# A softmax reciprocal moved from ScalarE to VectorE, and the evacuations of V moved the other way

## The chip, the cores and the metric

The kernel runs on one core of a Trainium2 chip. The metric is the device time of one execution in microseconds (us). Five engines work side by side on a core: TensorE (PE: matmuls, PEld: its weight loads), VectorE (DVE), ScalarE (ACT), GpSimd (POOL) and SyncE (SP, which issues most DMAs). Matmul results land in PSUM, eight banks of 128 partitions; everything else lies in SBUF.

## The reference

Two layers run one after the other on x of 2048 x 512. The first is an attention with a memory of 8 rows that is carried from one segment of 32 rows to the next:

```
for s in range(64):                       # 2048 / 32 segments, in sequence
    h = concat([mem, xs])                 # 8 + 32 = 40 rows of the layer-normed x
    q, k, v = h @ Wq, h @ Wk, h @ Wv      # 32 heads of 128
    scores = where(mask, q @ k.T * scale, -1e9)
    p = softmax(scores)
    o = (p @ v) @ Wo
    mem = o[:8]; outs.append(o[8:])
h = x + concat(outs)
```

The second is a gated MLP: `z = gelu(layernorm(h) @ w_in)`, split into z1 and z2, `g = w_sp @ layernorm(z2) + b_sp`, and `out = h + (z1 * g) @ w_out`. The change concerns only the softmax of the first.

## The kernel before

The program is one list of operations, written out in order; each engine executes its own in that order. A small emitter records what each operation reads and writes and puts in the waits. PSUM banks are tracked as a whole: an operation that writes a bank waits for every earlier reader of it on another engine.

The loop over the 64 segments (lines 896 to 1025) cannot overlap the segments freely, since the memory rows that one segment makes are input to the next. Within a segment the 32 heads are done in two halves of 16, b = 0 and 1. The order on TensorE is:

1. Q and K of both halves (`QK`, L481), with ScalarE copying each result out (L488) and VectorE transposing it in blocks (L494, L497).
2. `S_half(0)`: the scores of half 0 into bank 0 (L511, L520, L526). ScalarE takes the exponential (`sm_exp`, L534) without subtracting a maximum: a constant shift is added instead.
3. `V_half(0)`: V of half 0 (L575) into bank 6, then `sm_sums(0)`: matmuls with a block matrix of ones (L541, L546) put the sums of the exponentials, repeated over the partitions of a head group, into columns 224 to 383 of bank 0.
4. `S_half(1)` into bank 1, three of the four steps of `V_half(1)` (bank 2), `sm_sums(1)` into bank 1, and the last step of `V_half(1)`.
5. One group of work from a queue `gx` (L411 or L430, or later `z2_group`, L735). These are projections for the memory rows of later segments, or early parts of the second layer; they need nothing of this segment and fill the time until P is normalised. For one segment, s = 48, no such group is left.
6. `PV_half(0)` and `PV_half(1)` (L592, L598). Each of them writes all four banks 0, 1, 6 and 7.
7. The context copies `cT_evac` (ScalarE L611, VectorE L613), the output projection (L625, and L676 for the other rows), and the new memory rows (L649, L654).

The reciprocal of the sums is made on ScalarE in two operations, a logarithm (`sm_ln`, L553, from PSUM) and an exponential of its negative (`sm_rcp`, L557). VectorE then multiplies it into the exponentials in two operations, 160 and 64 elements wide (`sm_norm`, L561 and L566). Both normalisations stand behind both V evacuations in the program. `V_evac(0)` is a VectorE copy (L584), `V_evac(1)` a ScalarE copy (L582). The factor 2^-64 in the logarithm, and the constants beside it, keep numbers in range; `UNSC` takes it out again in `cT_evac`.

Of the kernel before, what the change touches and what calls it, by code (L numbers as in the profile page):

```python
# [9 lines left out]
ACT = mybir.ActivationFunctionType  # L10
ALU = mybir.AluOpType
# [158 lines left out]
def fast_path(nc, st, keep, A_x, A_mem0, A_Wq, A_Wk, A_Wv, A_Wo, A_seg_len, B_w_in, B_w_sp, B_b_sp, B_w_out, out):  # L170
# [17 lines left out]
    scale = float(DH) ** -0.5  # L188
    EPS = 1e-5
    SHIFT = 44.0  # L190
    NEG = -1.0e30
    RBIAS = 44.42
    LNS = 2.0 ** -64
    RK = math.exp(-RBIAS)

    em = Emitter(n_dma_sems=40)

    def sb(name, shape, dt):
        return st.enter_context(nc.sbuf_tensor("f_" + name, shape, dt))
# [25 lines left out]
    E_sb = sb("E_sb", [128, 2, 224], BF)  # L225
    R_sb = sb("R_sb", [128, 2, 160], F32)
# [9 lines left out]
    ones = sb("ones", [128, 128], BF)  # L236
# [23 lines left out]
    ps = st.enter_context(nc.psum_tensor("f_ps", [128, 8, 512], F32))  # L260
# [5 lines left out]
    def PB(b):  # L266
        return ("ps", b)
# [4 lines left out]
    def pe(fn, **k):  # L272
        return em.add("pe", fn, **k)

    def act(fn, **k):
        return em.add("act", fn, **k)

    def dve(fn, **k):
        return em.add("dve", fn, **k)

    def pool(fn, **k):
        return em.add("pool", fn, **k)
# [40 lines left out]
    def late_consts():  # L323
        pool(lambda e: e.memset(ones[:], 0.0), writes=["ones"])
        pool(lambda e: e.memset(Sc[:], 0.0), writes=["Sc"])
        pool(lambda e: e.memset(mask[:], 0.0), writes=["mask"])
        for c in range(4):
            q = slice(32 * c, 32 * c + 32)
            pool(lambda e, q=q: e.memset(ones[q, q], 1.0), writes=["ones"])
            pool(lambda e, q=q: e.affine_select(out=G_sb[q, :], in_=onesrc[q, 0:M], pattern=[[-1, M]], compare_op=ALU.is_equal,  # L330
                                                fill=0.0, base=0, channel_multiplier=1), reads=["onesrc"], writes=["G"])
            pool(lambda e, q=q: e.affine_select(out=F_sb[q, :], in_=onesrc[q, 0:32], pattern=[[-1, 32]], compare_op=ALU.is_equal,
                                                fill=0.0, base=-M, channel_multiplier=1), reads=["onesrc"], writes=["F"])
            pool(lambda e, q=q: e.affine_select(
                out=Sc[q, :].rearrange("p (s r) -> p s r", r=32)[:, :, XM:32], in_=onesrc[q, 0:32].rearrange("p (s r) -> p s r", r=8),
                pattern=[[-8, 4], [-1, 8]], compare_op=ALU.is_equal, fill=0.0, base=0, channel_multiplier=1),
                reads=["onesrc"], writes=["Sc"])
            m1 = mask[q, 0:160].rearrange("p (g t) -> p g t", t=40)[:, :, 16:40]
            pool(lambda e, m1=m1: e.affine_select(out=m1, in_=m1, pattern=[[0, 4], [1, 24]], compare_op=ALU.is_ge,
                                                  fill=NEG, base=8, channel_multiplier=-1), reads=["mask"], writes=["mask"])  # L340
            m2 = mask[q, 160:224].rearrange("p (g t) -> p g t", t=16)
            pool(lambda e, m2=m2: e.affine_select(out=m2, in_=m2, pattern=[[-8, 4], [0, 16]], compare_op=ALU.is_ge,
                                                  fill=NEG, base=0, channel_multiplier=1), reads=["mask"], writes=["mask"])
            pool(lambda e, m2=m2: e.affine_select(out=m2, in_=m2, pattern=[[8, 4], [0, 16]], compare_op=ALU.is_ge,
                                                  fill=NEG, base=7, channel_multiplier=-1), reads=["mask"], writes=["mask"])
            m3 = m2[:, :, 0:8]
            pool(lambda e, m3=m3: e.affine_select(out=m3, in_=m3, pattern=[[8, 4], [1, 8]], compare_op=ALU.is_ge,
                                                  fill=NEG, base=0, channel_multiplier=-1), reads=["mask"], writes=["mask"])
# [32 lines left out]
    def slot(s):  # L381
        return s % NSLOT
# [154 lines left out]
    def sm_sums(b):  # L537
        bank = SBK[b]
        for c in range(4):
            q = slice(32 * c, 32 * c + 32)  # L540
            pe(lambda e, q=q, c=c: e.matmul(ps[q, bank, 224:384], lhsT=ones[:, q], rhs=E_sb[:, b, 0:160], start=True, stop=False,  # L541
                                            skip_group_check=True, tile_position=(0, 32 * c)),
               reads=[("E", b), "ones"], writes=[PB(bank)])
        for c in range(4):
            q = slice(32 * c, 32 * c + 32)
            pe(lambda e, q=q, c=c: e.matmul(ps[q, bank, 224:384].rearrange("p (g q) -> p g q", q=40)[:, :, 0:16], lhsT=ones[:, q],  # L546
                                            rhs=E_sb[:, b, 160:224].rearrange("p (g q) -> p g q", q=16), start=False, stop=True,
                                            skip_group_check=True, tile_position=(0, 32 * c)),
               reads=[("Ex", b), "ones"], writes=[PB(bank)])

    def sm_ln(b):
        bank = SBK[b]
        act(lambda e: e.activation(out=R_sb[:, b, :], in_=ps[:, bank, 224:384], func=ACT.Ln, scale=LNS),  # L553
            reads=[PB(bank)], writes=[("R", b)])

    def sm_rcp(b):
        act(lambda e: e.activation(out=R_sb[:, b, :], in_=R_sb[:, b, :], func=ACT.Exp, scale=-1.0, bias=RBIAS),  # L557
            reads=[("R", b)], writes=[("R", b)])

    def sm_norm(b):  # L560
        dve(lambda e: e.scalar_tensor_tensor(out=E_sb[:, b, 0:160], in0=R_sb[:, b, :], scalar=RK, in1=E_sb[:, b, 0:160],  # L561
                                             op0=ALU.mult, op1=ALU.mult),
            reads=[("R", b), ("E", b)], writes=[("E", b)])
        ev = E_sb[:, b, 160:224].rearrange("p (g q) -> p g q", q=16)
        rv = R_sb[:, b, :].rearrange("p (g q) -> p g q", q=40)[:, :, 0:16]
        dve(lambda e: e.scalar_tensor_tensor(out=ev, in0=rv, scalar=RK, in1=ev, op0=ALU.mult, op1=ALU.mult),  # L566
            reads=[("R", b), ("Ex", b)], writes=[("Ex", b)])

    def V_half(s, b, dcs=range(DC)):
        bank = VB[b]  # L570
        sl = slot(s)
        for dc in dcs:
            for c in range(4):
                c0 = (16 * b + 4 * c) * DH
                pe(lambda e, dc=dc, c=c, c0=c0: e.matmul(ps[32 * c:32 * c + 32, bank, :], lhsT=hT[:, sl, dc, :], rhs=w_v[:, dc, c0:c0 + 512],  # L575
                                                         start=(dc == 0), stop=(dc == DC - 1), tile_position=(0, 32 * c)),
                   reads=[("hTx", (s // 4) % 3), ("hTm", s, dc // 2), ("W", 2, 2 * b), ("W", 2, 2 * b + 1)], writes=[PB(bank)])

    def V_evac(b, eng):
        bank = VB[b]  # L580
        if eng == "act":
            act(lambda e: e.activation(out=V_sb[:, b, :], in_=ps[:, bank, :], func=ACT.Copy), reads=[PB(bank)], writes=[("V", b)])  # L582
        else:
            dve(lambda e: e.tensor_copy(out=V_sb[:, b, :], in_=ps[:, bank, :]), reads=[PB(bank)], writes=[("V", b)])  # L584
# [16 lines left out]
                start=False, stop=True, skip_group_check=True, tile_position=(32 * c, 0)),  # L601
                reads=[("Vx", xb), ("Ex", b)], writes=[PB(PVB[c])])

    UNSC = 2.0 ** -64


    def cT_evac(c, eng):
        src = ps[:, PVB[c], 0:320]
        dst = cT[:, c, :]
        if eng == "act":  # L610
            act(lambda e: e.activation(out=dst, in_=src, func=ACT.Copy, scale=UNSC), reads=[PB(PVB[c])], writes=[("cT", c)])  # L611
        else:
            dve(lambda e: e.tensor_scalar(out=dst, in0=src, scalar1=UNSC, scalar2=None, op0=ALU.mult),  # L613
                reads=[PB(PVB[c])], writes=[("cT", c)])
# [180 lines left out]
    def start_v(n):  # L795
        start_group(vx_mm, vx_evac, 0, n)
# [99 lines left out]
    for s in range(NSEG):  # L896
# [31 lines left out]
            for n in range(2, 4):  # L928
                start_v(n)
        V_half(s, 0)  # L930
        V_evac(0, "dve")
        sm_sums(0)
        sm_ln(0)
        S_half(s, 1)
        lastop["s"] = em.by_eng["pe"][-1]
        sm_exp(1)
        sm_rcp(0)
        if s == 0:
            for n in range(4, 8):
                start_v(n)  # L940
        V_half(s, 1, (0, 1, 2))
        sm_sums(1)
        sm_ln(1)
        sm_rcp(1)
        V_half(s, 1, (3,))
        lastop["v"] = em.by_eng["pe"][-1]
        if s == NSEG - 1:
            sp(lambda e: e.dma_start(w_in1, winr[:, :, 0:FH]), writes=["w_in1"], after=[lastop["s"], lastop["x"]])
            xn2T_dma(11, [lastop["s"], lastop["x"]])
            z2_back(0, 7, lastop["v"])  # L950
        V_evac(1, "act")
        sm_norm(0)
        sm_norm(1)
        if s + 1 < NSEG:
            qx_copy(s + 1)
            lastop["x"] = em.by_eng["pool"][-1]
# [6 lines left out]
        ev = [gx.pop(0)()] if gx else [z2_group()] if zx and s > 3 * CK else []  # L963
# [148 lines left out]
    def zbank():  # L1112
        zcnt[0] += 1
        return 5 + zcnt[0] % 3
# [22 lines left out]
    for k, rb in enumerate(range(NP, RB)):  # L1137
# [18 lines left out]
        if k in (2, 3):  # L1156
            r, j, bank = RB - 4 + k, (k - 1) % 2, zbank()
# [45 lines left out]
    for tb in range(NTB):  # L1203
        for fb in range(len(ACC) if tb == 0 else 0, FB):
            if tb == 0:
                bank = 5 + fb % 3
            else:
                bank = gcnt % 2
# [785 lines left out]
```

## Time and profile before

| | |
|---|---|
| median of 3 runs | 885.25 us (884.95 to 886.3) |
| the profiled execution | 887.59 us, span 885.8 us |
| mean granted clock of TensorE | 0.994 |
| busy share: PE, DVE, ACT, POOL | 97%, 55%, 52%, 12% |
| reciprocal on ACT (L553, L557) | 128 x 305 ns and 128 x 333 ns |
| normalisation on DVE (L561, L566) | 128 x 325 ns and 128 x 221 ns |
| V copy on DVE (L584), on ACT (L582) | 64 x 692 ns; 580 ns at 410.07 us |

Times in the profile count from the start of the span. A row of the timeline gives the start, the duration, the engine, the line of the program, the operation, what it writes and reads, and in brackets how long its engine had been idle before it and what it then waited for. A row of the groups gives a line's total busy time, the mean of one in ns, and the idle time before. A row of the windows gives, for a stretch of time, its length, the busy time of each engine with the number of instructions, the granted clock of TensorE as a share of full speed, the busy share of the DMA engines and the GB/s that they moved.

### The profile page before, as it was taken

To read this page: it belongs to the slowest core of one execution; us is meant where nothing else is said; L and a number is where in the kernel's file an instruction comes from. 1 tells how busy PE (TensorE), PEld (TensorE's weight loads), DVE (VectorE), ACT (ScalarE), POOL (GpSimd) and SP (SyncE) were. 2 spreads that over 40 slices of the span, in tenths; PEclk is the share of its full clock that TensorE was granted. 3 is DMA by queue.
4 is the path that set the end of the run, shared out by engine and by line. 5 is a ranking of instruction groups with operands and counts; after the bars stand their busy time and mean duration, and the time that the engine had idled before them with its cause. 6 is when DMAs were issued, how large, how long until landed. Compare 5 with 4: busy or idle time off the path is not lost.

```text
span 885.8 us, 46595 instructions
## 1 busy us (share of the span) xinstructions
PE 858.6 (97%) x21446; PEld 488.5 (55%) x21453; DVE 487.6 (55%) x1128; ACT 457.3 (52%) x1147; POOL 110.6 (12%) x280
## 2 busy tenths in 40 slices
PE   6889999999999999999999999999999998999997
PEld 6645555565566655656565555555555543444443
DVE  3445556565556556565655565556555557364343
ACT  2346565666665656666665666466665575400000
POOL 1420111111111111010101011111101013200000
PEclk9999999999999999999999999999999999999999
DMA  9962232123320311211312121523222299032101
GB/s 320 377 177 63 64 57 61 44 59 63 60 58 25 84 46 32 65 45 52 60 43 52 46 66 47 102 69 78 73 62 67 62 244 333 2 101 76 62 13 38
DMA packets 109210, 76.35 MB, mean 86 GB/s; under 512 B 64104, under 2 KB 94512, under 8 KB 109008
## 3 DMA queue, kind: packets, MB, share of 16 engines
q1 hardware_dynamic: 108496, 73.04, 30.1%
q8 instruction: 170, 2.79, 1.3%
q14 instruction: 32, 0.26, 0.1%
q0 software_dynamic: 192, 0.20, 0.1%
q10 hardware_dynamic: 320, 0.07, 0.0%
HBM read 41.75 MB, written 20.91 MB: 71 GB/s over the span
## 4 chain that ended last, share of the span: by engine, by line
PE 94%; DVE 2%; issue 1%; DMA 1%; POOL 1%; ACT 0%; DVEq 0%
PE f_ps L481 26%; PE f_ps L625 13%; PE f_ps L575 12%; PE f_ps L1099 11%; PE f_ps L411 7%; PE f_ps L676 4%; PE f_ps L592 3%; PE f_ps L430 3%; PE f_ps L1188 3%; PE f_ps L1092 2%; PE f_ps L735 2%; PE f_ps L520 2%; PE f_ps L541 1%; PE f_ps L511 1%; PE f_ps L649 1%
## 5 line engine op out<-in xcount | busy, mean ns | idle before, releaser
L481 PE MATMUL f_ps<-f_arena,f_hT 128*32 128x512 bf16 x4096 | 240.3, 380 | 0.5 <-issue 0.2
L488 ACT ACTIVATE f_Tst<-f_ps 128x512 bf16<-128x512 f32 x256 | 145.9, 596 | 78.1 <-PE f_ps L481 77.9
L481 PEld LDWEIGHTS f_ps<-f_arena,f_hT 128*32 128x32 bf16 x4096 | 92.9, 96 | 104.0 <-ACT f_hT L654 32.7
L575 PE MATMUL f_ps<-f_arena,f_hT 128*32 128x512 bf16 x2048 | 140.4, 378 | 0.0
L625 PE MATMUL f_ps<-f_arena,f_cT 128*32 128x256 bf16 x4096 | 129.2, 274 | 0.9 <-ACT f_cT L611 0.8
L625 PEld LDWEIGHTS f_ps<-f_arena,f_cT 128*32 128x32 bf16 x4096 | 101.2, 97 | 21.7 <-ACT f_cT L611 18.7
L494 DVE STREAM_TRANSPOSE f_QT<-f_Tst 128x256 uint32<-128x256 uint32 x128 | 57.0, 446 | 91.7 <-ACT f_Tst L488 91.7
L1099 PE MATMUL f_ps<-f_arena 128*128 128x512 bf16 x448 | 100.9, 382 | 0.0
L613 DVE TENSOR_SCALAR f_cT<-f_ps 128x320 bf16<-128x320 f32 x128 | 56.9, 487 | 41.2 <-PE f_ps L598 41.2
L1099 PEld LDWEIGHTS f_ps<-f_arena 128*128 128x128 bf16 x448 | 44.1, 99 | 53.9 <-issue 2.2
L497 DVE STREAM_TRANSPOSE f_KT<-f_Tst 128x256 uint32<-128x256 uint32 x128 | 57.0, 445 | 29.1 <-ACT f_Tst L488 26.4
L411 PE MATMUL f_ps<-f_hTe,f_arena 128*128 128x128 bf16 x1024 | 68.0, 225 | 4.0 <-DVE f_arena L422 2.9
L611 ACT ACTIVATE f_cT<-f_ps 128x320 bf16<-128x320 f32 x128 | 49.0, 435 | 38.4 <-PE f_ps L598 38.4
L411 PEld LDWEIGHTS f_ps<-f_hTe,f_arena 128*128 128x128 bf16 x1024 | 60.3, 101 | 14.1 <-issue 9.5
L504 POOL COPY f_QT<-f_arena 128x256 bf16<-128x256 bf16 x64 | 30.7, 479 | 298.2 <-PE f_ps L526 298.1
L561 DVE SCALAR_TENSOR_TENSOR f_E_sb<-f_R_sb,f_E_sb 128x160 bf16<-128x160 f32 x128 | 41.7, 325 | 46.2 <-ACT f_R_sb L557 46.2
L642 DVE CAST f_part<-f_ps 128x256 bf16<-128x256 f32 x64 | 27.2, 425 | 68.9 <-PE f_ps L625 68.9
L553 ACT ACTIVATE f_R_sb<-f_ps 128x160 f32<-128x160 f32 x128 | 39.0, 305 | 37.9 <-PE f_ps L546 37.9
L575 PEld LDWEIGHTS f_ps<-f_arena,f_hT 128*32 128x32 bf16 x2048 | 45.2, 95 | 21.1
L1105 DVE TENSOR_TENSOR f_arena<-f_ps,f_arena 128x512 f32<-128x512 f32 x28 | 19.3, 690 | 60.7 <-PE f_ps L1099 60.7
L654 ACT ACTIVATE f_hT<-f_ps 128x16 bf16<-128x16 f32 x126 | 23.2, 184 | 55.1 <-PE f_ps L649 54.7
L633 POOL COPY f_cTx<-f_cT 128x256 bf16<-128x256 bf16 x64 | 25.6, 400 | 197.1 <-DVE f_cT L613 197.1
(113 smaller groups left out, 1165.8 us busy)
## 6 DMA issues: line engine op xcount, KB each, us to landing
wT_d<-f_wst SPq DMA_DIRECT2D x32, 256.0 KB, 2.3
f_arena<-wT_d SPq DMA_DIRECT2D x32, 256.0 KB, 5.1
f_arena<-in_A_Wq_dram SPq DMA_DIRECT2D x4, 1024.0 KB, 8.8
f_arena<-in_A_Wk_dram SPq DMA_DIRECT2D x4, 1024.0 KB, 14.2
f_arena<-in_A_Wv_dram SPq DMA_DIRECT2D x4, 1024.0 KB, 14.8
f_arena<-in_A_Wo_dram SPq DMA_DIRECT2D x4, 1024.0 KB, 13.6
f_Vx<-vext_d SPq DMA_DIRECT2D x62, 64.0 KB, 2.8
vext_d<-f_Vs SPq DMA_DIRECT2D x24, 128.0 KB, 2.0
```

Source lines behind the costliest of these rows:

```text
L411: pe(lambda e, h=h, dc=dc, hh=hh: e.matmul(ps[:, bank, hh * 128:(hh + 1) * 128], lhsT=ws[:, dc, h * DH:(h + 1) * DH], rhs=hTe[:, ck % 3, d ...
L481: pe(lambda e, dc=dc, c=c, rhs=rhs: e.matmul(ps[32 * c:32 * c + 32, bank, :], lhsT=hT[:, sl, dc, :], rhs=rhs, start=(dc == 0), stop=(dc == ...
L488: act(lambda e: e.activation(out=Tst[:, tb, :].rearrange("p (hp i r) -> p hp i r", i=32, r=2), in_=ps[:, bank, :].rearrange("p (hp r i) -> ...
L494: dve(lambda e: e.transpose(out=dst, in_=src), reads=[("T", tb)], writes=[("QT", b)])
L497: dve(lambda e: e.transpose(out=dst, in_=src), reads=[("T", tb)], writes=[("KT", b)])
L553: act(lambda e: e.activation(out=R_sb[:, b, :], in_=ps[:, bank, 224:384], func=ACT.Ln, scale=LNS), reads=[PB(bank)], writes=[("R", b)])
L561: dve(lambda e: e.scalar_tensor_tensor(out=E_sb[:, b, 0:160], in0=R_sb[:, b, :], scalar=RK, in1=E_sb[:, b, 0:160], op0=ALU.mult, op1=ALU.m ...
L575: pe(lambda e, dc=dc, c=c, c0=c0: e.matmul(ps[32 * c:32 * c + 32, bank, :], lhsT=hT[:, sl, dc, :], rhs=w_v[:, dc, c0:c0 + 512], start=(dc ...
L611: act(lambda e: e.activation(out=dst, in_=src, func=ACT.Copy, scale=UNSC), reads=[PB(PVB[c])], writes=[("cT", c)])
L613: dve(lambda e: e.tensor_scalar(out=dst, in0=src, scalar1=UNSC, scalar2=None, op0=ALU.mult), reads=[PB(PVB[c])], writes=[("cT", c)])
L625: pe(lambda e, h=h, g=g, i=i, b=b, c=c: e.matmul(ps[32 * g:32 * g + 32, bank, 0:d1 - d0], lhsT=cTh[:, i, 8:40], rhs=w_o[:, h, d0:d1], star ...
L1099: pe(lambda e: e.matmul(ps[:, bank, 0:TB], lhsT=z2[:, sc, fb * 128:(fb + 1) * 128], rhs=wTb[tb % 2][:, :, sc, :], start=(n == 0), stop=(n ...
```

## The change

The two ScalarE operations of the reciprocal become one VectorE `reciprocal`, which reads the sums from PSUM. It is issued right behind the sums of its half, and the normalisation of each half follows it at once instead of standing behind the V evacuations. `V_evac(0)` moves from VectorE to ScalarE. The second half of V is issued in one piece, ahead of the second sums. The scaling constants change: the ones matrix holds 2^-40, and the normalisation is a plain product.

```diff
-    RBIAS = 44.42
-    LNS = 2.0 ** -64
-    RK = math.exp(-RBIAS)
+    SUMS = 2.0 ** -40
+    UNSC = SUMS
...
-            pool(lambda e, q=q: e.memset(ones[q, q], 1.0), writes=["ones"])
+            pool(lambda e, q=q: e.memset(ones[q, q], SUMS), writes=["ones"])
...
-    def sm_ln(b):
+    def sm_rcp(b):
         bank = SBK[b]
-        act(lambda e: e.activation(out=R_sb[:, b, :], in_=ps[:, bank, 224:384], func=ACT.Ln, scale=LNS),
-            reads=[PB(bank)], writes=[("R", b)])
-
-    def sm_rcp(b):
-        act(lambda e: e.activation(out=R_sb[:, b, :], in_=R_sb[:, b, :], func=ACT.Exp, scale=-1.0, bias=RBIAS),
-            reads=[("R", b)], writes=[("R", b)])
+        dve(lambda e: e.reciprocal(out=R_sb[:, b, :], in_=ps[:, bank, 224:384]), reads=[PB(bank)], writes=[("R", b)])
 
     def sm_norm(b):
-        dve(lambda e: e.scalar_tensor_tensor(out=E_sb[:, b, 0:160], in0=R_sb[:, b, :], scalar=RK, in1=E_sb[:, b, 0:160],
-                                             op0=ALU.mult, op1=ALU.mult),
+        dve(lambda e: e.tensor_tensor(out=E_sb[:, b, 0:160], in0=R_sb[:, b, :], in1=E_sb[:, b, 0:160], op=ALU.mult),
...
-        dve(lambda e: e.scalar_tensor_tensor(out=ev, in0=rv, scalar=RK, in1=ev, op0=ALU.mult, op1=ALU.mult),
+        dve(lambda e: e.tensor_tensor(out=ev, in0=rv, in1=ev, op=ALU.mult),
...
-    UNSC = 2.0 ** -64
...
         V_half(s, 0)
-        V_evac(0, "dve")
+        V_evac(0, "act")
         sm_sums(0)
-        sm_ln(0)
+        sm_rcp(0)
         S_half(s, 1)
         lastop["s"] = em.by_eng["pe"][-1]
         sm_exp(1)
-        sm_rcp(0)
+        sm_norm(0)
...
-        V_half(s, 1, (0, 1, 2))
+        V_half(s, 1)
         sm_sums(1)
-        sm_ln(1)
         sm_rcp(1)
-        V_half(s, 1, (3,))
+        sm_norm(1)
         lastop["v"] = em.by_eng["pe"][-1]
...
         V_evac(1, "act")
-        sm_norm(0)
-        sm_norm(1)
```

## The prediction

> **What bounds the kernel now.** I read the page first (busy shares, then the chain that ended last), then the timeline of one segment in the steady part, then the groups of VectorE operations by shape, and last the windows around the few places where TensorE stands still.
>
> ```profile
> span 885.8 us, 46595 instructions
> PE 858.6 (97%) x21446; PEld 488.5 (55%) x21453; DVE 487.6 (55%) x1128; ACT 457.3 (52%) x1147; POOL 110.6 (12%) x280
> PE 94%; DVE 2%; issue 1%; DMA 1%; POOL 1%; ACT 0%; DVEq 0%
> ```
>
> TensorE is busy for 97% of the span and is 94% of the last chain. VectorE and ScalarE idle for almost half of it. So relief of ScalarE buys nothing by itself, and a change inside the segment costs only what it adds between two matmuls that now follow each other. The profiled execution lasted 887.59 us with a span of 885.8; it lies 2.34 us (0.3%) above the median of 885.25, so I work out a difference and add it to the median. About 0.2% (1.8 us) is what a measurement can tell from no change.
>
> The softmax of one segment, from the first sums to the second half of P·V (columns: start, duration, engine, line):
>
> ```profile
> 400.44 0.20 PEld L592 LDWEIGHTS f_ps<-f_E_sb,f_V_sb 32*128 32x128 bf16 x16
> ...
> 408.21 0.20 PE L546 MATMUL f_ps<-f_E_sb,f_ones 128*32 128x64 bf16 x4
> 408.32 0.69 DVE L584 CAST f_V_sb<-f_ps 128x512 bf16<-128x512 f32 x1
> 408.46 0.30 ACT L553 ACTIVATE f_R_sb<-f_ps 128x160 f32<-128x160 f32 x1 [0.39 <-PE f_ps L546]
> 408.75 0.36 ACT L534 ACTIVATE f_E_sb<-f_ps 128x224 bf16<-128x224 f32 x1
> 409.00 0.33 ACT L557 ACTIVATE f_R_sb<-f_R_sb 128x160 f32<-128x160 f32 x1
> 409.26 0.39 PE L575 MATMUL f_ps<-f_arena,f_hT 128*32 128x512 bf16 x4
> 409.36 0.33 DVE L561 SCALAR_TENSOR_TENSOR f_E_sb<-f_R_sb,f_E_sb 128x160 bf16<-128x160 f32 x1 [0.35 <-ACT f_R_sb L557]
> 409.49 0.31 ACT L553 ACTIVATE f_R_sb<-f_ps 128x160 f32<-128x160 f32 x1 [0.17 <-PE f_ps L546]
> 409.59 1.07 PE L411 MATMUL f_ps<-f_hTe,f_arena 128*128 128x128 bf16 x16
> 409.61 0.22 DVE L566 SCALAR_TENSOR_TENSOR f_E_sb<-f_R_sb,f_E_sb 128x64 bf16<-128x64 f32 x1
> 409.83 0.34 ACT L557 ACTIVATE f_R_sb<-f_R_sb 128x160 f32<-128x160 f32 x1
> 410.07 0.58 ACT L582 ACTIVATE f_V_sb<-f_ps 128x512 bf16<-128x512 f32 x1
> 410.20 0.33 DVE L561 SCALAR_TENSOR_TENSOR f_E_sb<-f_R_sb,f_E_sb 128x160 bf16<-128x160 f32 x1 [0.37 <-ACT f_R_sb L557]
> 410.44 0.22 DVE L566 SCALAR_TENSOR_TENSOR f_E_sb<-f_R_sb,f_E_sb 128x64 bf16<-128x64 f32 x1
> 410.58 0.17 PEld L592 LDWEIGHTS f_ps<-f_E_sb,f_V_sb 32*128 32x128 bf16 x16
> 410.81 0.20 PEld L592 LDWEIGHTS f_ps<-f_E_sb,f_V_sb 32*128 32x128 bf16 x16
> ```
>
> The first row is the same step one segment earlier: 10.37 us before the last row. The last normalisation ends at 410.66 and the second P·V half, which needs it, loads its weights at 410.81. The cover is the projection group of L411, until 410.66. That is a fit with about 0.04 us to spare once a handoff of 0.11 us is counted:
>
> ```profile
> 569.44 0.22 DVE L566 SCALAR_TENSOR_TENSOR f_E_sb<-f_R_sb,f_E_sb 128x64 bf16<-128x64 f32 x1
> 569.77 0.20 PEld L592 LDWEIGHTS f_ps<-f_E_sb,f_V_sb 32*128 32x128 bf16 x16 [0.20 <-DVE f_E_sb L566]
> 410.94 0.21 PE L598 MATMUL f_ps<-f_E_sb,f_Vx 32*128 32x64 bf16 x4
> 411.26 0.89 DVE L613 TENSOR_SCALAR f_cT<-f_ps 128x320 bf16<-128x320 f32 x2 [0.60 <-PE f_ps L598]
> ```
>
> VectorE to TensorE: 569.66 to 569.77, 0.11 us. TensorE to VectorE: 411.15 to 411.26, 0.11 us.
>
> **The edits with one answer.** Other values of the constants cost nothing. The normalisation keeps its element counts (160 and 64), so the pair keeps its 0.47 us (409.36 to 409.83). The first V evacuation moves to ScalarE: 0.69 us leave VectorE, 0.58 us join ScalarE in front of the second exp. V's first half was done before 408.32, where its copy started, so that exp would start near 408.9 instead of 408.75 and end near 409.26. V's second half in one piece issues the same matmuls, and the second sums now stand behind its fourth step: they end near 409.65, where that step ended (409.26 + 0.39), so the later exp is hidden by that step. If it were not, about 0.1 us a segment would be lost, and only if nothing later sets the end. Nothing of SP or POOL moves.
>
> **The reciprocal.** This is the whole price, and this trace has no such operation. The nearest rows by shape are VectorE's:
>
> ```profile
> L584 DVE CAST f_V_sb<-f_ps 128x512 bf16<-128x512 f32 x64 | 44.3, 692 | 1.2 <-PE f_ps L575 0.2
> L642 DVE CAST f_part<-f_ps 128x256 bf16<-128x256 f32 x64 | 27.2, 425 | 68.9 <-PE f_ps L625 68.9
> L1076 DVE BATCH_NORM_AGGREGATE f_mv<-f_st 128x2 f32<-128x12 f32 x16 | 3.3, 209 | 0.6
> L692 DVE BATCH_NORM_AGGREGATE f_mv<-f_stats 128x2 f32<-128x6 f32 x16 | 2.9, 182 | 0.5
> ```
>
> A copy out of PSUM takes (692-425)/256 = 1.04 ns an element and 158 ns fixed. At that price a reciprocal of 160 elements takes R = 0.33 us: the lower end. The aggregate is the one row in which each number passes through several dependent steps: 27 ns for six more numbers, 4.5 ns a number, or 13.5 ns for each set of three if a set is the unit that the steps run through. A quotient to float32's precision is such dependent work, not a copy, so I take the value between these two, their geometric mean of 7.8 ns an element: R = 0.158 + 160 x 0.0078 = 1.41 us. The ends for the range are 0.33, 0.88 (4.5 ns) and 2.32 us (13.5 ns).
>
> [...]
>
> **The new chain.** Before, ScalarE's logarithm and exponential ran beside VectorE. Now everything queues on VectorE, in program order: reciprocal 0, pair 0, reciprocal 1, pair 1. The first sums end at 408.41, so reciprocal 0 starts at 408.52. With 0.03 us between a producer and its reader (409.33 to 409.36 in the rows of L557 and L561), pair 0 ends at 409.02 + R, reciprocal 1 ends at 409.02 + 2R and pair 1 at 409.52 + 2R; the second P·V half starts at 409.63 + 2R instead of 410.81. The shift is 2R - 1.18 us, and it is positive from R = 0.59 on. With 1.41 it is 1.64 us. Behind the waiting reciprocal 1 stand pair 1 and VectorE's two context copies; TensorE waits for all of them, since the first P·V half also writes bank 1, where reciprocal 1 still reads its sums. 64 segments (the x64 of L584) give 105 us.
>
> **What is late next: the clock.** TensorE would stand still from 410.66 to 411.95, run the first P·V half (0.23 us), and stand still again to 412.45: 1.56 us idle in every segment. The trace of before has one segment with such a hole:
>
> ```profile
> 555.71 0.21 PE L598 MATMUL f_ps<-f_E_sb,f_Vx 32*128 32x64 bf16 x4
> 556.48 0.17 PE L592 MATMUL f_ps<-f_E_sb,f_V_sb 32*128 32x40 bf16 x1 [0.56 <-DVE f_E_sb L566]
> 557.41 0.27 PE L592 MATMUL f_ps<-f_E_sb,f_V_sb 32*128 32x40 bf16 x15 [0.76 <-issue]
> ...
> 401.37 1.70 PE L625 MATMUL f_ps<-f_arena,f_cT 128*32 128x256 bf16 x56
> 558.28 3.17 PE L625 MATMUL f_ps<-f_arena,f_cT 128*32 128x256 bf16 x56
> ...
> 557.00:558.00 1.00, 0.59 (x27) 0.31 (x27) 0.17 (x1) 0.24 (x1) 0.00 (x0) 0.94 0.70 190
> 558.00:559.00 1.00, 1.00 (x24) 0.62 (x20) 0.72 (x2) 0.53 (x2) 0.22 (x1) 0.50 2.07 286
> 561.00:562.00 1.00, 0.91 (x32) 0.48 (x27) 0.22 (x1) 0.18 (x1) 0.00 (x0) 0.86 0.36 81
> ```
>
> After 0.56 + 0.76 = 1.32 us idle the granted clock (third figure from the end of a window's row) fell to 0.50, and the same 56 matmuls took 3.17 instead of 1.70 us. Means of 0.94 and 0.86 in the outer windows put the half clock at 557.88 to 561.28: 3.40 us, which cost up to 1.70. I read this as a clock judged in stretches of 3.40 us and lowered for the next one. A second place bounds the idle time that it takes:
>
> ```profile
> 733.43 1.90 PE L1092 MATMUL f_ps<-f_arena 128*128 128x512 bf16 x8 [1.06 <-ACT f_arena L1063]
> 732.00:734.00 2.00, 0.94 (x8) 0.50 (x7) 1.91 (x5) 1.81 (x4) 0.06 (x2) 1.00 1.22 376
> 736.00:738.00 2.00, 0.52 (x3) 0.29 (x4) 1.89 (x7) 0.00 (x0) 1.41 (x3) 1.00 0.90 259
> 738.00:740.00 2.00, 2.00 (x8) 0.76 (x7) 1.97 (x5) 0.72 (x2) 0.18 (x1) 0.69 1.01 380
> ```
>
> There 1.06 us idle left the clock at 1.00; it fell only near 738.8, after a longer hole. So the limit lies between 1.06 and 1.32 us in 3.40; I take 1.19. The hole, 1.79 us long with its 0.23 of work, lies wholly in one stretch for 3.40 - 1.79 = 1.61 us of start positions. A stretch may also miss 0.37 us of it at the front, or 0.60 at the back with the first P·V half, and still hold 1.19 idle. That is 2.58/3.40 = 0.76 of the segments (0.61 at 1.32, 0.84 at 1.06), if positions are spread evenly. Each pays 1.70 us, as the work after the hole is matmul after matmul: 0.76 x 1.70 x 64 = 83 us.
>
> Sum: 105 + 83 = 188 us, 885.25 + 188 = **1073 us**. With the reciprocals VectorE does more, but no other wait of TensorE's moves: after pair 1 the order of both is the old one.
>
> **Rivals.** (1) *The hole costs only itself.* The clock holds at 1.00, or the price is below mine: 885.25 + 105 = 990 us; at R = 0.88 the shift is 0.58 and the time 922. For it: only a few holes in the trace show a drop, and the one at 556 fell into heavy transfers. Against: the drop there has the right length and follows a smaller hole. [...]
>
> (2) *The reciprocal is as cheap as a copy.* Below R = 0.59 nothing is late. With 0.33, counted from the second sums at 409.65: 409.76 + 0.33 + 0.03 + 0.47 + 0.11 = 410.70, before 410.81. In the few late segments where L592 already waits 0.20 us, up to 0.07 us each is gained, and if the hole at 556 shrinks under the limit its 1.70 us go too: 883 to 885 us, not slower. For it: shape and place are a copy's. Against: the dependent steps above. [...]
>
> (3) *Each set's 13.5 ns is the price of an element.* R = 2.32, shift 3.46: 221 us, and every segment pays the clock, 109 us: 1215 us.
>
> **How the numbers follow.** The forecast 0.60; rival 1 0.25; rival 2 0.11; rival 3 0.04. Rivals 2 and 3 are left out of the range. Its low end is rival 1 with the price halfway between 0.88 and 1.41 us (R = 1.15, shift 1.12, 72 us: 957). Its high end takes the arithmetic mean of 4.5 and 13.5, 9.0 ns an element: R = 1.60, shift 2.02, 129 us; the hole then lowers the clock in 0.87 of the segments by the same count, 95 us: 1109. Slower gets 0.60 + 0.25 + 0.04 = 0.89; rival 2 is split into 0.05 faster (the hole at 556 goes) and 0.06 the same.
>
> **What would show it.** A row RECIPROCAL x128 with a mean near 1400 ns; L592 waiting on VectorE for about 1.6 us a segment; segments near 13.3 us on average where they took 10.37; clock digits of 7 to 9 through the loop instead of 9; VectorE's busy time up from 488 to about 624 us (+180 for the reciprocals, -44 for L584). A mean below 590 ns makes the forecast wrong at its root; a mean near 1400 with the clock at 1.00 makes it rival 1.

## The result, and the profile after

The changed kernel took 940.59 us (median of 5 runs, 939.53 to 942.27); the kernel before, beside it, 884.95 us. The ratio is 1.063 (95% interval 1.061 to 1.065). The change makes the kernel 55.6 us slower. The direction was forecast; the size, 1073 us, was not, and 940.6 lies below the forecast range of 957 to 1109.

The page after, in its parts (span, busy shares, granted clock in 40 slices, chain that ended last, and the groups that answer to L553, L557 and L592 of before):

```profile
span 937.8 us, 46411 instructions
PE 868.8 (93%) x21453; PEld 497.8 (53%) x21453; DVE 585.6 (62%) x1192; ACT 422.0 (45%) x955; POOL 110.4 (12%) x280
PEclk9999999999999999999999999999999999999999
PE 73%; DVE 22%; issue 2%; DMA 1%; POOL 1%; ACT 0%; DVEq 0%
L552 DVE RECIPROCAL f_R_sb<-f_ps 128x160 f32<-128x160 f32 x128 | 147.8, 1155 | 10.8 <-PE f_ps L545 10.8
L585 PE MATMUL f_ps<-f_E_sb,f_V_sb 32*128 32x40 bf16 x2048 | 46.8, 178 | 45.5 <-DVE f_R_sb L552 36.1
```

VectorE was on 2% of the chain and is now on 22%. The reciprocal took 1155 ns, not the 305 + 333 ns of the two ScalarE operations. The granted clock shows a 9 in every slice and its mean is 0.994, as before, so almost nothing was lost there. One segment of the timeline after, from the end of the first sums to the second P·V half:

```profile
402.21 0.20 PE L545 MATMUL f_ps<-f_E_sb,f_ones 128*32 128x64 bf16 x4
402.47 1.16 DVE L552 RECIPROCAL f_R_sb<-f_ps 128x160 f32<-128x160 f32 x1 [0.16 <-PE f_ps L545]
403.44 0.20 PE L545 MATMUL f_ps<-f_E_sb,f_ones 128*32 128x64 bf16 x4
403.58 1.07 PE L410 MATMUL f_ps<-f_hTe,f_arena 128*128 128x128 bf16 x16
403.67 0.33 DVE L555 TENSOR_TENSOR f_E_sb<-f_R_sb,f_E_sb 128x160 bf16<-128x160 f32 x1
404.04 1.15 DVE L552 RECIPROCAL f_R_sb<-f_ps 128x160 f32<-128x160 f32 x1
404.58 0.19 PE L585 MATMUL f_ps<-f_E_sb,f_V_sb 32*128 32x40 bf16 x1
405.23 0.33 DVE L555 TENSOR_TENSOR f_E_sb<-f_R_sb,f_E_sb 128x160 bf16<-128x160 f32 x1
405.25 0.17 PEld L585 LDWEIGHTS f_ps<-f_E_sb,f_V_sb 32*128 32x128 bf16 x15 [0.58 <-DVE f_R_sb L552]
405.67 0.20 PEld L585 LDWEIGHTS f_ps<-f_E_sb,f_V_sb 32*128 32x128 bf16 x16 [0.23 <-issue]
...
415.26 1.15 DVE L552 RECIPROCAL f_R_sb<-f_ps 128x160 f32<-128x160 f32 x1
```

The two reciprocals stand one behind the other with the products between them. One matmul of the first P·V half starts (it writes bank 0), the other 15 wait for the second reciprocal, which still reads bank 1. The second half starts 3.26 us after the sums ended (402.41 to 405.67), where it took 2.40 before (408.41 to 410.81): 0.86 us. The second reciprocal of the next segment follows 11.22 us later, against 10.37 us a segment before. If every segment is like this one, 64 x 0.85 = 54.4 of the 55.6 us are in this one place; where the other 1.2 us are is open.

### The profile page after: what moved, and what is told of

It reads as the page before. It is cut to its first block, busy times and chain, and to the rows that moved or that the text cites. A ratio compares the mean times of both kernels' runs of the same rounds, so it can differ in the third digit from the quotient of the medians.

```text
span 937.8 us, 46411 instructions
## 1 busy us (share of the span) xinstructions
PE 868.8 (93%) x21453; PEld 497.8 (53%) x21453; DVE 585.6 (62%) x1192; ACT 422.0 (45%) x955; POOL 110.4 (12%) x280
## 4 chain that ended last, share of the span: by engine, by line
PE 73%; DVE 22%; issue 2%; DMA 1%; POOL 1%; ACT 0%; DVEq 0%
PE f_ps L480 24%; DVE f_R_sb L552 15%; PE f_ps L617 12%; PE f_ps L1088 10%; PE f_ps L568 6%; PE f_ps L668 4%; PE f_ps L1177 3%; DVE f_E_sb L559 2%; DVE f_E_sb L555 2%; PE f_ps L1081 2%; PE f_ps L410 2%; PE f_ps L429 2%; PE f_ps L585 2%; PE f_ps L540 1%; PE f_ps L641 1%
## 5 line engine op out<-in xcount | busy, mean ns | idle before, releaser
L480 PE MATMUL f_ps<-f_arena,f_hT 128*32 128x512 bf16 x4096 | 240.9, 380 | 0.5 <-issue 0.3
L552 DVE RECIPROCAL f_R_sb<-f_ps 128x160 f32<-128x160 f32 x128 | 147.8, 1155 | 10.8 <-PE f_ps L545 10.8
L568 PE MATMUL f_ps<-f_arena,f_hT 128*32 128x512 bf16 x2048 | 132.9, 378 | 0.0
L575 ACT ACTIVATE f_V_sb<-f_ps 128x512 bf16<-128x512 f32 x128 | 76.4, 597 | 45.3 <-PE f_ps L568 45.3
L585 PE MATMUL f_ps<-f_E_sb,f_V_sb 32*128 32x40 bf16 x2048 | 46.8, 178 | 45.5 <-DVE f_R_sb L552 36.1
L410 PE MATMUL f_ps<-f_hTe,f_arena 128*128 128x128 bf16 x1024 | 67.4, 224 | 3.6 <-DVE f_arena L421 2.8
L585 PEld LDWEIGHTS f_ps<-f_E_sb,f_V_sb 32*128 32x128 bf16 x2048 | 29.2, 91 | 71.0 <-DVE f_R_sb L552 42.2
L410 PEld LDWEIGHTS f_ps<-f_hTe,f_arena 128*128 128x128 bf16 x1024 | 59.7, 100 | 8.0 <-DVE f_arena L421 3.0
```

The lines of the kernel that those rows point to most:

```text
L410: pe(lambda e, h=h, dc=dc, hh=hh: e.matmul(ps[:, bank, hh * 128:(hh + 1) * 128], lhsT=ws[:, dc, h * DH:(h + 1) * DH], rhs=hTe[:, ck % 3, d ...
L480: pe(lambda e, dc=dc, c=c, rhs=rhs: e.matmul(ps[32 * c:32 * c + 32, bank, :], lhsT=hT[:, sl, dc, :], rhs=rhs, start=(dc == 0), stop=(dc == ...
L552: dve(lambda e: e.reciprocal(out=R_sb[:, b, :], in_=ps[:, bank, 224:384]), reads=[PB(bank)], writes=[("R", b)])
L585: pe(lambda e, q=q, c=c, g=g, c0=c0: e.matmul(ps[:, PVB[c], c0:c0 + 40], lhsT=V_sb[q, b, g * 128:(g + 1) * 128], rhs=E_sb[q, b, g * 40:(g ...
```

## The experiments

The theory after the result: the loss is the serial chain on VectorE. The second P·V half starts 2R + 0.95 us after the first sums, and TensorE waits for what exceeds the 2.40 us of before; a shift of 2R - 1.45 us a segment. The rivals: the V edits carry a part of the loss; or each reciprocal has a cost of its own, whatever it delays. And the prediction's clock term was untested, since the hole in the changed kernel is only about 0.62 us (0.48 us before the 15 matmuls, 0.14 us behind them).

**The reciprocal edit without the V edits.** In the changed kernel:

```diff
-        V_evac(0, "act")
+        V_evac(0, "dve")
...
-        V_half(s, 1)
+        V_half(s, 1, (0, 1, 2))
         sm_sums(1)
         sm_rcp(1)
+        V_half(s, 1, (3,))
         sm_norm(1)
```

> VectorE reciprocals and their places as in the change, but V's first copy back on VectorE and V's second half again in three steps, sums, one step. Serial chain (the second P.V half waits for two reciprocals and the products one after the other on VectorE, 2R + 0.95 us after the first sums): the 0.69 us copy now stands ahead of the first reciprocal, which starts about 0.53 us later; shift 0.86 + 0.53 = 1.39 us a segment, 89 us, about 974 us; if the clock's limit is as predicted, up to 50 us more. Rival (the V edits carry part of the loss): below 940 us.

Measured: 969.38 us, ratio to the kernel before 1.093 (1.091 to 1.095). Its timeline:

```profile
397.18 0.20 PE L545 MATMUL f_ps<-f_E_sb,f_ones 128*32 128x64 bf16 x4
397.29 0.69 DVE L577 CAST f_V_sb<-f_ps 128x512 bf16<-128x512 f32 x1
397.90 1.15 DVE L552 RECIPROCAL f_R_sb<-f_ps 128x160 f32<-128x160 f32 x1
```

The V copy now holds up the first reciprocal by 0.52 us after the sums, against 0.06 in the changed kernel. That is 0.46 x 64 = 29 us, the 28.8 us by which this kernel is slower than the change. So the V edits do not carry the loss. They take a third off what the reciprocal edit alone costs (83 us over the 886.27 beside it).

**The V edits without the reciprocal edit.** In the kernel before:

```diff
-        V_evac(0, "dve")
+        V_evac(0, "act")
...
-        V_half(s, 1, (0, 1, 2))
+        V_half(s, 1)
         sm_sums(1)
         sm_ln(1)
         sm_rcp(1)
-        V_half(s, 1, (3,))
```

> The kernel before with only the V edits: first V copy on ScalarE, V's second half in one piece, logarithm and exponential still on ScalarE. Serial chain: ScalarE now has 0.58 us more ahead of the logarithms, its last V copy ends near 411.25 on the clock of the predicted segment where P.V started at 410.81, so about 0.45 us a segment, 29 us, 914 us; the V edits then help only once the reciprocal has left ScalarE. If the V edits are free in either setting: 885 us. Rival (the V edits carry most of the loss of the change): 930 us or more.

Measured: 900.45 us, where the kernel before took 886.27 (ratio 1.016, 1.015 to 1.018). The mechanism is as expected, at half the price. ScalarE had been idle for 0.39 us before the first logarithm (the row at 408.46 in the prediction), and part of the copy falls into that time: the logarithm starts 0.41 us after the first sums instead of 0.05, so the copy delays it by 0.36 us and not by 0.58. With the logarithms still on ScalarE and the V copy in front of them, the V edits cost 14 us (some 3 of them may be V's second half in one piece, below). Neither part of the change is free alone.

**Fewer columns.** The reciprocals of the changed kernel over the first 80 or 120 of 160 columns; the others hold a constant.

```diff
-        dve(lambda e: e.reciprocal(out=R_sb[:, b, :], in_=ps[:, bank, 224:384]), ...
+        dve(lambda e: e.reciprocal(out=R_sb[:, b, 0:80], in_=ps[:, bank, 224:304]), ...
```

> The change, with the reciprocals over 80 of the 160 columns; the other 80 columns of the reciprocals hold a constant, so half of the probabilities are not normalised by their sums. With 6.25 ns an element and 155 ns fixed, R = 0.66 us, 2R + 0.95 = 2.26 us, below the 2.40 us that were there before: no wait is left, 885 us within 2. Rival (V edits or their order carry part of the loss): above 890 us.

> The same with 120 of 160 columns; the other 40 hold a constant. R = 0.905 us, shift 2 x 0.905 - 1.45 = 0.36 us a segment, 23 us: 908 us. If a reciprocal's price were mostly fixed, R would stay near 1.1 us and the time near 935.

Measured: 910.0 us with 120 columns, +23.7 us on the 886.27 beside it, where +23 was expected. With 80 columns 889.75 us, ratio 1.0041 (1.0023 to 1.0059): the wait is gone, and 3.5 us are left. The groups of the two runs:

```profile
L553 DVE RECIPROCAL f_R_sb<-f_ps 128x80 f32<-128x80 f32 x128 | 84.1, 657 | 15.5 <-PE f_ps L546 10.8
L553 DVE RECIPROCAL f_R_sb<-f_ps 128x120 f32<-128x120 f32 x128 | 115.7, 904 | 11.0 <-PE f_ps L546 11.0
```

657, 904 and 1155 ns for 80, 120 and 160 columns are 6.2 ns an element and 159 ns fixed. The fixed part is that of a copy out of PSUM (158 ns), the part per element about six times a copy's 1.04 ns.

**The 3.5 us that were left.** The 80-column kernel with V's second half back in three steps, sums, one step.

```diff
-        V_half(s, 1)
+        V_half(s, 1, (0, 1, 2))
         sm_sums(1)
         sm_rcp(1)
+        V_half(s, 1, (3,))
         sm_norm(1)
```

> The 80-column reciprocals again (the other 80 columns hold a constant), with V's second half back in three steps, sums, one step. The 80-column run came out 3.5 us above the kernel before, where no wait was expected. If issuing V's second half in one piece costs those 3.5 us (about 0.05 us a segment), this run is at the kernel before within 1 us. If they come from VectorE's chain (2R + 0.95 being a little more than 2.40), it stays 3 to 4 us above.

Measured: 886.66 us against 885.82, ratio 1.0004 (0.9991 to 1.0017). Nothing is left. So issuing V's second half in one piece does cost a little where no longer wait hides it; why is open.

**Half 1 back on ScalarE.** The changed kernel, half 0 with the VectorE reciprocal, half 1 with logarithm and exponential (`sm_rcp_act` and `sm_norm_act` are the operations of before).

```diff
-        V_half(s, 1)
+        V_half(s, 1, (0, 1, 2))
         sm_sums(1)
-        sm_rcp(1)
-        sm_norm(1)
+        sm_rcp_act(1)
+        V_half(s, 1, (3,))
+        sm_norm_act(1)
```

> The change with half 1 alone put back to logarithm and exponential on ScalarE (and V's second half in three steps, sums, one step); half 0 keeps the VectorE reciprocal. Serial chain: reciprocal 0 and its products end about 1.6 us after the first sums, long before they are needed, and half 1 is as before: 885 us within 2. Rival (each VectorE reciprocal costs its own share): half of the loss, about 913 us.

Measured: 885.79 us against 885.16, ratio 1.001 (0.9996 to 1.0024). 64 reciprocals of 1.16 us are still there, 74 us of VectorE time, and cost nothing that can be measured. So a reciprocal on VectorE costs nothing where nothing waits for it; the loss comes with the second one. How much of it is the queue behind the first can be estimated from the rows of the changed kernel. The second sums end at 403.64 and the second reciprocal starts at 404.04; alone on VectorE it would start 0.06 us after the sums, as the first one does, and so 0.34 us earlier. The other 0.52 of the 0.86 us would stay, since a single reciprocal behind the second sums is already longer than its cover. No run has the reciprocal of half 1 alone on VectorE.

**A longer hole.** The changed kernel with one more reciprocal of n columns ahead of the second, or with both doubled (then `for x in (0, 1)` stands around the reciprocal itself).

```diff
+        for x in ((0,) if b else ()):
+            dve(lambda e: e.reciprocal(out=R_sb[:, b, 0:n], in_=ps[:, bank, 224:224 + n]), ...
         dve(lambda e: e.reciprocal(out=R_sb[:, b, :], in_=ps[:, bank, 224:384]), ...
```

> The change with one more reciprocal of 64 columns ahead of the second one, written to the place that the second one overwrites. R of 64 columns is 0.56 us. Without the clock: 0.56 x 64 = 36, 976 us. TensorE's idle time in the hole grows from 0.62 to about 1.2 us, at the limit of 1.06 to 1.32 that the prediction read; with the clock lowered in up to half of the segments up to 50 us more, 1026.

> The change with the second reciprocal done twice. Without the clock: 1.16 x 64 = 74, 1015 us. The idle time in the hole grows to about 1.8 us; by the predicted reading of the clock three of four segments run 3.40 us at half clock, 83 us more, 1098 us.

> The change with both reciprocals done twice. Without the clock: 2.31 x 64 = 148, 1089 us. [...]

Measured: 978.32, 1090.98 and 1137.96 us. With 64 columns the chain alone explains the time: the next reciprocal starts 0.58 us later, 64 x 0.58 = 37, 978. (Two of its four runs took 981 us at a mean granted clock of 0.991, two 976 at 0.996: the difference is about 10 us at half clock.) With 160 columns it is 1.19 us later, 1017 without the clock; 74 us more were lost. With both doubled 1093, and 45 us more. The granted clock in 40 slices, for 64, for 160, and for both doubled:

```profile
PEclk9999999999999999999999999999999999999999
PEclk9998898989889898989889898889889889999999
PEclk9988898999999989989989989988899899999999
```

The clock does fall, and it falls less often for the longest hole (mean granted clock 0.916 for 160, 0.936 for both doubled). Read in stretches, all changes of the clock with both doubled, from 189 to 503 and from 701 to 902 us, lie on a grid of 3.41 us. There the stretches with up to 1.65 us idle had kept the clock and 12 of the 15 above had lost it, which put the limit far above the prediction's. The next run decides at the very hole that the prediction had forecast.

> The change with one more reciprocal of 115 columns (0.87 us) ahead of the second one. TensorE's idle time in the hole is then about 1.54 us, what the prediction had forecast for the change. By the predicted reading of the clock (limit 1.19 us of idle time in a stretch of 3.40) three of four segments are lowered: 940.6 + 64 x 0.88 + 80 = 1077 us. If the limit is near half of the stretch, 1.65 to 1.9, as the runs with longer holes show it, no segment is lowered: 997 us.

Measured: 1078.92 us, the prediction's reading, not the later one. The next reciprocal starts 0.90 us later, 998 us without the clock; 81 us more were lost. In its trace the clock is halved for 54 stretches between 69 and 910 us (its mean of 0.913 over 1077.0 us is 187 us at half clock), so that is 1.50 us for each. Six of its stretches on the grid:

```profile
414.27:417.68 3.41, 1.87 (x66) 1.29 (x62) 2.90 (x7) 0.64 (x3) 0.00 (x0) 1.00 0.02 5
417.68:421.10 3.42, 3.42 (x72) 2.58 (x67) 1.19 (x3) 1.28 (x4) 0.40 (x1) 0.50 0.00 0
421.10:424.51 3.41, 3.41 (x84) 1.49 (x80) 2.51 (x6) 1.45 (x4) 0.79 (x2) 1.00 0.16 50
...
431.33:434.74 3.41, 3.41 (x64) 2.35 (x59) 1.34 (x3) 0.94 (x3) 0.40 (x1) 0.50 0.02 5
...
322.12:325.53 3.41, 1.87 (x76) 1.30 (x79) 2.90 (x7) 0.77 (x2) 0.14 (x1) 1.00 0.39 119
325.53:328.95 3.42, 3.42 (x104) 1.90 (x100) 1.60 (x4) 1.09 (x4) 0.84 (x3) 1.00 0.10 24
```

The first stretch is 1.87 us busy, 1.54 idle; the next has the clock at 0.50 for all of it, and the one after is back at 1.00. So here the clock changes at the ends of these stretches and holds for the whole of one. The next half clock, at 431.33, follows four stretches, 13.65 us, behind the one at 417.68. A segment with a halved stretch lasts about as long (13.77 us from the first reciprocal at 399.06 to that at 412.83), so its hole falls on nearly the same place of the grid as the one before: from 200 to 517 and from 712 to 853 us, 23 of the 24 halved stretches that have one ahead of them there stand four stretches behind it.

But the stretch at 322.12 is 1.87 busy too, and the clock behind it stays. In the same two parts of this run, 25 stretches at full clock with 1.54 to 1.79 us of idle time were followed by half clock, and seven with 1.40 to 1.54 were not; with both doubled, three with 1.68 to 1.83 were, and 43 with 1.36 to 1.75 were not. So idle time alone does not decide there. The two stretches also differ in the matmuls that they hold:

```profile
413.93 1.07 PE L410 MATMUL f_ps<-f_hTe,f_arena 128*128 128x128 bf16 x16
416.51 0.27 PE L587 MATMUL f_ps<-f_E_sb,f_V_sb 32*128 32x40 bf16 x15 [1.40 <-DVE f_R_sb L554]
417.65 0.62 PE L429 MATMUL f_ps<-f_arena,f_hTe 128*32 128x512 bf16 x4
...
323.56 0.27 PE L587 MATMUL f_ps<-f_E_sb,f_V_sb 32*128 32x40 bf16 x15 [1.40 <-DVE f_R_sb L554]
324.70 0.39 PE L429 MATMUL f_ps<-f_arena,f_hTe 128*32 128x512 bf16 x4
324.91 1.70 PE L619 MATMUL f_ps<-f_arena,f_cT 128*32 128x256 bf16 x56
```

The first holds 0.73 us of the group of L410 (128 x 128) and 0.03 us of L429; the second holds 0.83 us of L429 and L619. Whether this decides was not shown; no run was made to test it.

Why both doubled lost less, in two places of that run:

```profile
315.09:318.50 3.41, 1.88 (x37) 1.29 (x29) 3.34 (x5) 0.82 (x2) 0.33 (x1) 1.00 0.31 63
318.50:321.92 3.42, 2.00 (x83) 1.48 (x87) 2.91 (x7) 0.77 (x2) 0.32 (x1) 1.00 0.08 26
321.92:325.33 3.41, 3.41 (x115) 2.11 (x107) 0.64 (x2) 1.56 (x5) 0.09 (x1) 1.00 0.02 5
...
202.45:205.86 3.41, 0.67 (x10) 0.40 (x7) 3.34 (x5) 0.04 (x1) 0.00 (x0) 1.00 0.20 77
205.86:209.28 3.42, 3.27 (x79) 2.00 (x83) 1.96 (x6) 0.77 (x2) 0.40 (x1) 0.50 0.02 5
```

At 315 to 322 the grid cuts the hole in two, 1.53 and 1.42 us idle, and neither half lowers the clock. At 202 one stretch holds 2.74 us, and it does. In this run segments of about 13.6 us, four stretches, then keep the hole at the same place of the grid for many segments. So what a hole lost to the clock here depended on where the grid cuts it, and not on its length alone.

**A cover for segment 48.** In the kernel before, for the hole that the prediction had read at 556:

```diff
+        if s == 3 * CK:
+            WoX_mm(rb - 1, j4)
         PV_half(s, 0)
         PV_half(s, 1)
...
         if rb > 0:
-            WoX_mm(rb - 1, j4)
+            if s != 3 * CK:
+                WoX_mm(rb - 1, j4)
```

> The kernel before with one group of eight matmuls (L676, 0.61 us, which need nothing of the segment) moved ahead of P.V in segment 48 only, the one segment without a cover. Its hole of 1.40 us idle in one stretch shrinks by 0.6, and about 0.5 us of waiting for the context copies opens behind P.V. If the half clock after it goes, 1.7 us are won: about 883.5 us; if not, no change within 0.5 us.

Measured: 885.04 us against 885.82, ratio 0.9993 (0.9977 to 1.0009): not told apart from no change. Its window of 550 to 560 shows the clock at 1.00, where the kernel before had 0.50 in part of it:

```profile
550.00:560.00 10.00, 8.96 (x283) 4.86 (x272) 5.90 (x16) 6.03 (x16) 1.67 (x4) 1.00 0.80 175
```

That does not show the cover at work. 0.76 us of the hole of before are a wait that the profile puts down to "issue" (the row at 557.41 in the prediction), and this trace has no such wait. And the 23 runs of the kernel before that stood beside it differ among themselves by more than one halved stretch: their mean granted clocks go from 0.995 to 0.998, 2.7 us of 884. Whether the cover saves the 1.7 us is open; they are below what the runs can tell. No version here beats the kernel before.

## Why the prediction was wrong

The forecast was 105 us for the chain and 83 us for the clock, 188; measured were 55.6 and nearly nothing. Three terms of the sum failed: the price of the reciprocal, the handoffs of the chain, and the clock, which hung on both.

**The price of the reciprocal** was taken at 1.41 us; it is 1.155. Two of them a segment: 2 x 0.255 x 64 = 33 us too much. The value lay between the two aggregate prices, 4.5 and 13.5 ns an element, at 6.2 ns; the geometric mean was the guess that failed. That the aggregate's price is one of dependent steps, and that a reciprocal shares it, was assumed; no run shows it.

**The handoffs of the chain** were summed to 1.22 us beside the two reciprocals, 0.95 measured. VectorE started 0.06 us after the sums, not 0.11; the second reciprocal started 0.09 us before the product ahead of it had ended; and the second P·V half waited for the wide product alone, not for the narrow one behind it, which only the last four matmuls read. All of it is 0.27 us a segment, 17 us. 105 - 33 - 17 = 55. The prediction had taken the last wait from the row at 569.77 of before, which the profile puts down to the narrow product. But the matmuls of that row read V as well, and its copy on ScalarE ended at 569.65, 0.01 us before the narrow product:

```profile
569.07 0.58 ACT L582 ACTIVATE f_V_sb<-f_ps 128x512 bf16<-128x512 f32 x1
```

By what the kernel lets them read, they waited for this copy, and the row said nothing of the narrow product.

**The clock** was the largest miss, 83 us, and it is missing mostly because the other two were too large: the hole is 0.62 us, not 1.56. With a hole of 1.54 us the run with 115 more columns lost 81 us to the clock, against 83 forecast. That the clock is lowered for a whole stretch of 3.4 us, the one behind the hole's, was right (0.50 from 417.68 to 421.10). That the sizes agree is in part luck, for two steps behind the 83 us were wrong. The positions of the holes are not spread evenly but repeat on the grid (54 halved stretches for 64 segments, at 1.50 us each, where 0.76 of the segments at 1.70 us were forecast). And the limit of 1.19 us was too low: in the run with 64 more columns, stretches with 1.22 us idle (at 356.61 and 380.50) kept the clock, and so did those with up to 1.46 us (at 745.73); of the stretches read on the grid, none lost it with less than 1.40. The prediction's upper bound of 1.32 was wrong as well, since it left out idle time of this stretch of before, 1.40 us in all:

```profile
554.47:557.88 3.41, 2.01 (x71) 1.01 (x64) 1.20 (x6) 1.79 (x6) 0.47 (x1) 1.00 1.28 216
```

The run with 64 more columns stands for two reciprocals of 1.44 us each, the predicted price within 2%, and it took 978 us, 12 us from rival 1. So even at the predicted price the measured handoffs would have kept the hole (0.62 + 0.51 = 1.13 us) below what lowered the clock in any of those stretches: the clock term of the forecast would have failed with its price right.

**What held.** The edits priced at nothing cost nothing that shows in the changed kernel; V in one piece would cost 3 us if no wait hid it. The point from which the price decides, R = 0.59 in the prediction, is 0.73 by the measured chain: 0.66 us (80 columns) leaves no wait, 0.90 us (120) does. That bank 1 holds back the first P·V half was right (L585 waits for L552). Rival 1's formula came nearest: with the measured price its shift is 1.13 us a segment, 957 us.

## What to carry to other kernels

An engine that is busy half of the time (VectorE, 55% before) is not free: what counts is the time between an operation's input and the work that waits for its result. Here the second P·V half was late by the length of the second reciprocal (by the estimate above 0.52 of 0.86 us) and by the queue behind the first (0.34). With the first on VectorE and the second on ScalarE the same work cost nothing. When a sum ends in a threshold, work out the threshold term at both ends of the terms ahead of it before it enters the forecast; here a hole forecast 0.94 us too long brought in 83 us that were not there. And where a wait has two possible causes that end 0.01 us apart, the profile's name for it decides nothing; what the waiting operation reads does.

## What the runs showed of the hardware

A VectorE reciprocal out of PSUM took 159 ns and 6.2 ns an element (657, 904 and 1155 ns for 80, 120 and 160 columns). TensorE's granted clock changed on a grid of 3.41 us and was halved for whole stretches of it (0.50 from 417.68 to 421.10, behind a stretch with 1.54 us idle, in the run with 115 more columns). Stretches of that run with 1.54 us idle went either way (lost behind that at 414.27, kept behind that at 322.12), and so did those with 1.68 to 1.75 us with both doubled; what else decides was not shown. A hole of about 2.94 us (0.62 and two reciprocals of 1.16) lost less to the clock (45 us) than one of 1.54 us (81 us): in one of the two places shown the grid cut it in two, while the shorter one met the grid at the same place in segment after segment.
